# Loading a weight matrix in two pieces of 16 and 112 partitions instead of one of 128

## The chip, the cores and the metric

The program runs on one core of a Trainium2 chip. The metric is the device time of one execution in microseconds (us). The kernel before takes 677.37 us, the median of three runs from 677.31 to 677.42.

## What is computed

One decoding step for a batch of two rows x of 448 values. The result mixes attention over a cache (16 heads of 256 values, 4096 positions) with a small feed-forward block, by a gate g:

```python
g = _sigmoid((x * gate_w).sum(-1, keepdims=True))
q = (x @ wq).reshape(B, Sq, H, Dh).transpose(0, 2, 1, 3)   # wq: 448 x 4096
scores = einsum("bhqd,bhkd->bhqk", q, k_cache) * (Dh ** -0.5)
a = einsum("bhqk,bhkd->bhqd", softmax(scores), v_cache) ... @ wo
r = relu(x @ w1 + b1); b = (r * r) @ w2 + b2
return g * a + (1 - g) * b
```

All data is float32. The two caches are 134 MB each, and the four weight matrices together 21 MB.

## The kernel before

The work is cut into 16 rounds; a round takes one batch row and two heads. Per round an 8.4 MB tile of the K cache is loaded into one of two buffers (`kp0`, `kp1`) and an 8.4 MB tile of the V cache into a third (`vp`), each as 128 partitions (rows of the on-chip memory) of 64 KB. VectorE (DVE) multiplies the K tile by q in place (line 445) and sums along each row (line 450), in two halves of 8.7 us each; a maximum, two exponentials on ScalarE (ACT) and 32 matmuls with V on TensorE (PE, `values`) follow.

Nearly all loads are issued by SyncE (SP), in program order, through `load` (line 273), which issues one `dma_start` and registers what it writes. SP waits, before each load, until the buffer is free: before a K tile for DVE, before a V tile for PE. The class `Flow` works these waits out from the named regions that each operation reads and writes, and every load has a semaphore of its own name.

The start of the program is what the change touches. Line 303 calls the first part of `vp` the tile `wq_t`: the 448 x 4096 matrix wq, laid out as 128 partitions of seven consecutive half rows, 14,336 values or 57,344 bytes, which are contiguous in the main memory too. Line 304 is SP's first load and brings in the whole of it; line 405 is the second and brings the K tile of round 0. ACT issues four small loads meanwhile (x, gate_w and b2 to two partitions each, and b1, line 325, to sixteen partitions of 448 bytes). On PE the order is: a turn of x (line 373), the gate (396), b2 (398), b1 (400), and then 28 matmuls x @ wq (line 427, drawn as 56 in the profile), which wait for wq. Their result is scaled into `qs` (line 428) and spread into the q of rounds 0 and 1 (`make_q`). Only after the wq matmuls may SP issue the load of w1, into the same place of `vp` (line 430); w1's matmuls (line 435) stand in the same way before the first V tile. At the end come the last V tile in three pieces, w2 in four pieces, and PE's closing matmuls.

Of the kernel before, what the change touches and what calls it, by code (L numbers as in the profile page):

```python
# [10 lines left out]
PE, ACT, DVE, POOL, SP = "PE", "ACT", "DVE", "POOL", "SP"  # L11
# [12 lines left out]
class Flow:  # L24
# [22 lines left out]
    def op(self, eng, fn, r=(), w=(), give=None, take=(), dma=None):  # L47
        proc = dma or eng
        looped = eng == PE and self.body is not None
        o = Op(proc, eng, fn, give, looped)  # L50
        mine = self.ops.setdefault(proc, [])
        mine.append(o)
        o.n = len(mine)
        know = self.know[eng]
        for t in take:
            p = self.tokens[t].pop(0)
            o.takes.append((t, 16 if p.proc not in self.eng else 1))
            self.learn(know, p)
        need = {}
        for writes, regions in ((False, r), (True, w)):  # L60
            for name, lo, hi in map(self.span, regions):
                for p, a, b, wrote in self.seen.setdefault(name, []):
                    if a >= hi or b <= lo or not (wrote or writes):
                        continue
                    if p.proc == proc == PE:
                        continue
                    if know.get(p.proc, 0) < p.n and need.get(p.proc, p).n <= p.n:
                        need[p.proc] = p
        for p in sorted(need.values(), key=lambda p: -p.n):
            if know.get(p.proc, 0) >= p.n:  # L70
                continue
            assert not looped, (eng, p.proc, p.n, r, w)
            while p.give and p.proc in self.eng:
                later = [q for q in self.ops[p.proc][p.n:] if not q.give and q is not o]
                assert later, (eng, p.proc, p.n, r, w)
                p = later[0]
            p.inc = True
            o.waits.append(p)
            self.learn(know, p)
        for writes, regions in ((False, r), (True, w)):  # L80
            for name, lo, hi in map(self.span, regions):
                at = self.seen.setdefault(name, [])
                if writes:
                    at[:] = [x for x in at if not (lo <= x[1] and x[2] <= hi)]
                at.append((o, lo, hi, writes))
        o.know = dict(know)
        if give:
            self.tokens.setdefault(give, []).append(o)
        if looped:
            if self.passes == 1:  # L90
                self.body.append(o)
            else:
                first = self.body[self.at]
                assert first.takes == o.takes and not o.waits, (first.takes, o.takes)
                self.at += 1
        else:
            self.order[eng].append(o)
        return o
# [84 lines left out]
def gated_mix_kernel(nc, x, k_cache, v_cache, wq, wo, w1, b1, w2, b2, gate_w, out):  # L183
    P = 128
    B, H, S, DH = k_cache.shape
    D = x.shape[-1]
    F = w1.shape[1]
    N = H * DH
    XR = 7
# [10 lines left out]
    QB = 512  # L200
    NQ = N // QB
# [4 lines left out]
    BUSY = (8, 12, 3, 1)  # L206
    SLOTS = (0, 16, 104)
    LEAD = 4
    HJ = HG * DH // P
    HP = P // HG  # L210
    HN = HG * DH
# [4 lines left out]
    op = flow.op  # L216

    def sb(name, *shape):
        return nc.alloc_sbuf_tensor(name, shape, F32).ap()

    def bank(name):
        return nc.alloc_psum_tensor(name, (P, 512), F32).ap()

    kp = [sb(f"kp{n}", P, NK * DH) for n in range(2)]
    vp = sb("vp", P, NK * DH)
    wo_t = sb("wo", P, HJ * D)
    b1T = sb("b1T", P, FC)
# [8 lines left out]
    xT = sb("xT", P, 2, XC, 2, B)  # L236
# [20 lines left out]
    rl_t = [sb(f"rl{n}", P, HG * B, 2) for n in range(2)]  # L257
    oTw = sb("oTw", P, HJ, B)
    oT2 = o2_w.rearrange("p (b j) -> p j b", b=B)[:, :HJ // 2, :]
    oTn = on_w.rearrange("p (b j k) -> p j k b", b=B, k=2)[:, :NJ, :, :]  # L260

    po_t = [bank(f"po{n}") for n in range(2)]
# [10 lines left out]
    def load(eng, sem, dst, src, w, r=(), give=None):  # L273
        e = flow.eng[eng]
        op(eng, lambda: e.dma_start(dst, src), r=r, w=w, dma=sem, give=give)  # L275

    def place(t, lo=0, hi=NK * DH):
        return ("vp" if t is vp else "kp1" if t is kp[1] else "kp0", lo, hi)
# [22 lines left out]

    by7 = "(r k) (s n) -> (r k s) n"
    wq_t = vp[:, :D * N // P]
    load(SP, "wq", wq_t, wq.rearrange(by7, k=XR, s=2).rearrange("(p k) n -> p (k n)", k=XR), [place(vp, 0, D * N // P)])

    start_at = kp[1][:B, :4 * D + XC * P]

# [58 lines left out]
    def mms(calls):  # L366
        def run():
            for out_, lhsT, rhs, start, stop in calls:
                i = t_.matmul(out_, lhsT, rhs, start=start, stop=stop, skip_group_check=True)  # L369
            return i  # L370
        return run

    op(PE, mms([(pxv[:, c, :], xr[:, c].rearrange("b r s -> b (r s)"), ident[:B, :B], True, True) for c in range(XC)]),
       r=[xr_r, "ident"], w=["sm"])
# [6 lines left out]
    def times_x(out_, t, width, n):  # L381
        calls = []
        for a in range(XR):
            c, half = divmod(a, 2)
            for k in range(n):
                calls.append((out_[32 * k:32 * k + 2 * B, :width], xT[:, half, c].rearrange("p s b -> p (s b)"),
                              t[:, (a * n + k) * width:(a * n + k + 1) * width], a == 0, a == XR - 1))
        return mms(calls)
# [35 lines left out]
        c = col(i)  # L424
        op(ACT, lambda: s_.activation(sel, c, AF.Copy), r=["ident"], w=["sel"], give="q")

    op(PE, times_x(po_t[1], wq_t, QB, NQ // 2), r=["xT", place(vp, 0, D * N // P)], w=["po1"])
    op(ACT, lambda: s_.activation(qs, po_t[1], AF.Copy, scale=scale), r=["po1"], w=["qs"])
    w1_t = vp[:, :D * F // P]
    load(SP, "w1", w1_t, w1.rearrange(by7, k=XR, s=2).rearrange("(p k) n -> p (k n)", k=XR), [place(vp, 0, D * F // P)])  # L430
# [5 lines left out]
    for k in range(FB // 2):  # L436
        op(ACT, lambda k=k: s_.activation(h_sb[:, k * D:(k + 1) * D], ph[32 * k:32 * k + 2 * B, :D], AF.Copy),
           r=["ph"], w=[("shared", k * D, (k + 1) * D)])
    load_k(1)

    def times_q(i, half, lo, hi):
        t, a, q = kp[i % 2], half * J, q_of[i]
        kt = rows(t)[:, a + lo:a + hi, :]
        at = [place(t, (a + lo) * DH, (a + hi) * DH)]
        vec(lambda: v_.tensor_tensor(kt, kt, q.unsqueeze(1).to_broadcast([P, hi - lo, DH]), op=ALU.mult), at + [f"q{i % 3}"], at)  # L445
# [14 lines left out]
    def maximum(i, token=False):  # L460
        s = s_t[i % 2]
        vec(lambda: v_.tensor_reduce(m, s, axis=AX.X, op=ALU.max), [f"s{i % 2}"], ["m"], give="m" if token else None)
        op(PE, mms([(mt[k * PH:(k + 1) * PH, :PH], m.to_broadcast([P, PH]), ident[:, k * PH:(k + 1) * PH], True, True)
                    for k in range(2)]), r=["m", "ident"], w=["mt"], take=["m"] if token else ())
# [56 lines left out]

    o_w = shared.rearrange("r (s j k p) -> r s j k p", s=2, j=HJ // 2, k=HG)

    def turn_wide(u):
        ptv = sm[:, :HJ * HG * B].rearrange("p (j c) -> p j c", c=HG * B)
        po, rl = po_t[0], rl_t[u % 2]
        pv = po.rearrange("r (s p j) -> r s j p", s=2, j=HJ)
        for lo in range(0, HJ, HJ // 2):
            for s in range(2):
                op(ACT, lambda s=s, lo=lo: s_.activation(o_w[:, s], pv[:, s, lo:lo + HJ // 2].unsqueeze(2).to_broadcast([P, HJ // 2, HG, HP]),  # L530
                                              AF.Copy), r=["po0"], w=[("shared", s * HN // 2, (s + 1) * HN // 2)])
            ov = o_w.rearrange("r s j k p -> r s j (k p)")
            op(PE, mms([(ptv[:, lo + j, :], ov[:, s, j, :], rl[:, :, s], s == 0, s == 1)
                        for j in range(HJ // 2) for s in range(2)]), r=["shared", f"rl{u % 2}"], w=["sm"])
        if u < NG - 2:
            op(ACT, lambda: s_.activation(po, zero.to_broadcast([P, 512]), AF.Copy), r=["zero"], w=["po0"])
        for k in range(HG):
            at = slice(k * HP, (k + 1) * HP)
            op(ACT, lambda k=k, at=at: s_.activation(oTw[at], ptv[at, :, B * k:B * k + B], AF.Copy), r=["sm"], w=[("oTw", k, k + 1)])  # L539
# [135 lines left out]
    maximum(i + 1)  # L675
    times_q(i + 2, 0, 0, LEAD)
    softmax(i + 1)
    times_q(i + 2, 0, LEAD, J)
    values(i, vt)
# [15 lines left out]
    maximum(i + 1)  # L695
    times_q(i + 2, 0, 0, LEAD)
    norm(NG - 1)
    softmax(i + 1)
    times_q(i + 2, 0, LEAD, J)
    values(i, vt)  # L700
# [61 lines left out]
```

## Time and profile before

| what | value |
|---|---|
| median of three runs | 677.37 us |
| the profiled execution, its own time | 677.36 us |
| its span, first to last instruction | 675.9 us |
| read from the main memory | 289.56 MB, 428 GB/s over the span |
| DVE busy | 571.4 us (85%) |
| PE busy | 252.1 us (37%) |
| ACT busy | 43.0 us (6%) |
| wq: from SP's issue to landing | 19.5 us |

Times in the rows are microseconds from the span's start, unless a column is marked ns. PE is TensorE's matmuls and PEld its weight loads; an engine's name with a q is its instruction queue, so SPq rows are loads being issued. Every helper that issues a matmul or a load has one line, so L369 is any matmul and L275 any load; the tile names tell them apart (`vp<-in_A_wq_dram` is wq into `vp`). In the sliced rows a digit is a busy share in tenths. The DMA share is the mean over the core's 16 DMA engines. A DMA packet is counted in the slice in which it starts, with all its bytes, so short windows show bursts.

### The profile page before, as it was taken

What the parts mean: (1) busy time and instruction counts of PE and PEld (TensorE: products, weight loads), DVE (VectorE), ACT (ScalarE), POOL (GpSimd) and SP (SyncE); (2) the same over time, 40 slices, a digit from 0 to 9 for tenths busy, and PEclk for the clock granted to TensorE, in tenths of its full rate; (3) what the DMA queues carried; (4) which work ended last, traced back from release to release, by engine and by line L of the source; (5) the groups of instructions that cost most, each with busy time, mean ns of one, the idle gap of its engine ahead of it and who ended that gap; (6) DMA issues with size and microseconds to landing.
All of it is one profiled execution on the core that took longest, in us unless ns stands there. A gap on an engine that the chain in (4) does not pass through costs nothing.

```text
span 675.9 us, 3913 instructions
## 1 busy us (share of the span) xinstructions
PE 252.1 (37%) x1716; PEld 87.3 (13%) x1716; DVE 571.4 (85%) x149; ACT 43.0 (6%) x143; POOL 0.7 (0%) x6
## 2 busy tenths in 40 slices
PE   2522350502305751140505455050421480421598
PEld 1100210100101510010101411010100140100223
DVE  3069999999999895979979896897979899999930
ACT  0001000000100201010000201000010110000000
POOL 0000000000000000000000000000000000000000
PEclk9956575665758567585856578565575856565789
DMA  9999999999999999999999999999999999999997
GB/s 381 430 434 435 435 434 434 434 434 435 434 434 434 423 435 434 430 434 434 434 434 434 442 431 434 434 434 430 427 430 434 418 468 430 430 431 434 397 434 316
DMA packets 6688, 289.73 MB, mean 429 GB/s; under 512 B 783, under 2 KB 917, under 8 KB 1557
## 3 DMA queue, kind: packets, MB, share of 16 engines
q1 hardware_dynamic: 6632, 289.55, 99.3%
q8 instruction: 9, 0.15, 0.1%
q10 hardware_dynamic: 44, 0.02, 0.0%
q14 instruction: 3, 0.02, 0.0%
HBM read 289.56 MB, written 0.01 MB: 428 GB/s over the span
## 4 chain that ended last, share of the span: by engine, by line
DMA 49%; DVE 31%; PE 3%; SPq 0%; issue 0%; DVEq 0%
DMA kp<-in_A_k_cache_dram 32%; DVE s L450 15%; DVE kp L445 15%; DMA vp<-in_A_v_cache_dram 11%; DMA kp<-in_B_w_dram 6%; PE po L369 3%; SPq L275 0%; PE fin L369 0%; PE mt L369 0%; DVE shared L733 0%; DVEq L155 0%; DVE nb L472 0%
## 5 line engine op out<-in xcount | busy, mean ns | idle before, releaser
L445 DVE TENSOR_TENSOR kp<-kp,q 128x8192 f32<-128x8192 f32 (+2 forms) x34 | 278.2, 8183 | 49.5 <-DMA kp<-in_A_k_cache_dram 49.5
L450 DVE TENSOR_REDUCE s<-kp 128x32 f32<-128x8192 f32 x32 | 277.9, 8686 | 1.1
L369 PE MATMUL po<-vp,pw 128*16 128x512 f32 (+1 forms) x960 | 135.9, 729 | 229.9 <-PEq L153 209.3
L369 PEld LDWEIGHTS po<-vp,pw 128*16 128x16 f32 (+1 forms) x960 | 31.0, 110 | 331.5 <-issue 307.9
L369 PE MATMUL mt<-ident,m 128*64 128x64 f32 x64 | 7.3, 318 | 140.5 <-PEq L153 86.7
L369 PE MATMUL sm<-rl,shared 128*128 128x8 f32 (+1 forms) x120 | 25.3, 348 | 9.4 <-ACT shared L530 8.1
L369 PEld LDWEIGHTS sm<-rl,shared 128*128 128x128 f32 x120 | 24.7, 313 | 11.6 <-DVE rl L503 4.6
L369 PE MATMUL acc<-wo,oTw 128*2 128x448 f32 x48 | 25.0, 687 | 2.5 <-ACT oTw L539 2.5
L369 PEld LDWEIGHTS mt<-ident,m 128*64 128x64 f32 x64 | 4.8, 191 | 154.4 <-issue 98.5
L491 ACT ACTIVATE pw<-zero 128x128 f32<-128x128 f32 x12 | 3.7, 311 | 326.1 <-PE po L369 326.1
L479 ACT ACTIVATE pw<-s,nb 64x64 f32<-64x64 f32 x32 | 11.1, 348 | 167.2 <-DVE nb L472 167.0
L733 DVE COPY shared<-fin 128x112 f32<-128x112 f32 x1 | 0.3, 275 | 20.1 <-PE fin L369 20.1
L369 PE MATMUL ph<-vp,xT 128*4 128x448 f32 x28 | 7.0, 664 | 16.8 <-DMA vp<-in_B_w_dram 16.8
L472 DVE TENSOR_REDUCE nb<-mt 128x1 f32<-128x64 f32 x16 | 3.6, 224 | 10.4 <-PE mt L369 10.4
L369 PE MATMUL pq<-qs,sel 128*64 128x256 f32 x48 | 12.3, 594 | 0.0
L369 PE MATMUL po<-kp,pw 128*8 128x512 f32 x64 | 10.0, 785 | 5.9 <-DMA kp<-in_A_v_cache_dram 5.9
L369 PE MATMUL po<-vp,xT 128*4 128x512 f32 x56 | 7.6, 699 | 1.4 <-DMA vp<-in_A_wq_dram 1.4
L421 ACT ACTIVATE q<-pq 128x256 f32<-128x256 f32 x16 | 6.1, 383 | 21.6 <-PE pq L369 21.4
L501 DVE RECIPROCAL rc<-sm 128x8 f32<-128x8 f32 (+1 forms) x5 | 1.0, 196 | 7.7 <-PE sm L369 7.7
L530 ACT ACTIVATE shared<-po 128x512 f32<-128x512 f32 x12 | 6.5, 591 | 11.4 <-PE sm L369 11.4
L369 PEld LDWEIGHTS acc<-wo,oTw 128*2 128x2 f32 x48 | 4.5, 99 | 20.7 <-issue 18.0
L369 PE MATMUL ph<-kp,ones_pp 128*16 128x512 f32 x48 | 6.7, 593 | 0.0
(77 smaller groups left out, 77.6 us busy)
## 6 DMA issues: line engine op xcount, KB each, us to landing
vp<-in_A_wq_dram SPq DMA_DIRECT2D x1, 7168.0 KB, 19.5
wo<-in_A_wo_dram SPq DMA_DIRECT2D x3, 1792.0 KB, 46.5
vp<-in_A_v_cache_dram SPq DMA_DIRECT2D x1, 4096.0 KB, 24.1
vp<-in_B_w_dram SPq DMA_DIRECT2D x1, 3136.0 KB, 19.1
vp<-in_A_v_cache_dram SPq DMA_DIRECT2D x1, 3072.0 KB, 31.0
wo<-in_A_wo_dram SPq DMA_DIRECT2D x2, 896.0 KB, 33.9
kp<-in_B_w_dram SPq DMA_DIRECT2D x1, 1792.0 KB, 36.9
vp<-in_A_v_cache_dram SPq DMA_DIRECT2D x1, 1024.0 KB, 33.1
```

What stands on the lines that cost most here:

```text
L369: i = t_.matmul(out_, lhsT, rhs, start=start, stop=stop, skip_group_check=True)
L421: op(ACT, lambda: s_.activation(t, pq[:, :DH], AF.Copy), r=["pq"], w=[f"q{i % 3}"])
L445: vec(lambda: v_.tensor_tensor(kt, kt, q.unsqueeze(1).to_broadcast([P, hi - lo, DH]), op=ALU.mult), at + [f"q{i % 3}"], at)
L450: vec(lambda: v_.tensor_reduce(s[:, at], rows(t)[:, at, :], axis=AX.X, op=ALU.add), [place(t, half * HALF, (half + 1) * HALF)], [(f"s{i % ...
L472: vec(lambda: v_.tensor_reduce(nb, mt[:, :PH], axis=AX.X, op=ALU.max, negate=True), ["mt"], [f"nb{i % 2}"])
L479: op(ACT, lambda: s_.activation(pw[at, :, 2 * c:2 * c + 2], s[at].rearrange("p (m s) -> p m s", s=2), AF.Exp, bias=nb[at], accum_out=rs[at ...
L491: op(ACT, lambda: s_.activation(at, zero.unsqueeze(2).unsqueeze(3).to_broadcast([P, NK // 2, 2, 2]), AF.Copy), r=["zero"], w=[("pw0", 2 * ...
L501: vec(lambda: v_.reciprocal(c, sm[:, :B * n].rearrange("p (k b) -> p k b", b=B)), ["sm"], ["rc"])
L530: op(ACT, lambda s=s, lo=lo: s_.activation(o_w[:, s], pv[:, s, lo:lo + HJ // 2].unsqueeze(2).to_broadcast([P, HJ // 2, HG, HP]), AF.Copy), ...
L733: vec(lambda: v_.tensor_copy(y4, fin[:, :DQ]), ["fin"], [("shared", 0, DQ)])
```

## The change

The one load of wq becomes two on the same queue, of the same 57,344 bytes per partition: partitions 0 to 15, and then partitions 16 to 127. Each has its own semaphore and its own region name, and the wq matmuls read both regions.

```diff
+    WQ_FIRST = 16
...
     wq_t = vp[:, :D * N // P]
-    load(SP, "wq", wq_t, wq.rearrange(by7, k=XR, s=2).rearrange("(p k) n -> p (k n)", k=XR), [place(vp, 0, D * N // P)])
+    wq_v = wq.rearrange(by7, k=XR, s=2).rearrange("(p k) n -> p (k n)", k=XR)
+    wq_at = [place(vp, 0, D * N // P)]
+    for lo, hi in ((0, WQ_FIRST), (WQ_FIRST, P)):
+        load(SP, f"wq{lo}", wq_t[lo:hi], wq_v[lo:hi], [f"wq{lo}"])
+        wq_at.append(f"wq{lo}")
...
-    op(PE, times_x(po_t[1], wq_t, QB, NQ // 2), r=["xT", place(vp, 0, D * N // P)], w=["po1"])
+    op(PE, times_x(po_t[1], wq_t, QB, NQ // 2), r=["xT", *wq_at], w=["po1"])
```

The head of SP's queue, in the order in which SP issues its loads, with partitions x values per partition, reads before:

```order
L275 DMA vp<-in_A_wq_dram 128x14336
L275 DMA kp<-in_A_k_cache_dram 128x16384
L275 DMA vp<-in_B_w_dram 128x6272 [waits s_PE]
L275 DMA kp<-in_A_k_cache_dram 128x16384 [waits s_DVE]
L275 DMA vp<-in_A_v_cache_dram 128x16384 [waits s_PE]
```

and now:

```order
L276 DMA vp<-in_A_wq_dram 16x14336
L276 DMA vp<-in_A_wq_dram 112x14336
L276 DMA kp<-in_A_k_cache_dram 128x16384
L276 DMA vp<-in_B_w_dram 128x6272 [waits s_PE]
L276 DMA kp<-in_A_k_cache_dram 128x16384 [waits s_DVE]
```

One load more stands at the head; what follows is in the same order behind the same waits (`in_B_w` is w1 here). On PE the first instructions, with the semaphores that they wait for, were:

```order
L369 MATMUL sm<-gd,ones_pp 128x4 [waits s_DVE]
L369 MATMUL acc<-kp,gd 2x448 [waits s_b2]
L369 MATMUL ph<-kp 128x112 [waits s_b1]
L369 MATMUL po<-vp,xT 4x512 [waits s_wq]
L369 MATMUL po<-vp,xT 4x512 x27
```

and are now:

```order
L374 MATMUL sm<-gd,ones_pp 128x4 [waits s_DVE]
L374 MATMUL acc<-kp,gd 2x448 [waits s_b2]
L374 MATMUL ph<-kp 128x112 [waits s_b1]
L374 MATMUL po<-vp,xT 4x512 [waits s_wq16,s_wq0]
L374 MATMUL po<-vp,xT 4x512 x27
```

The first wq matmul waits for two semaphores in place of one, and nothing changed its place. DVE, ACT and GpSimd have the same instructions in the same order.

## The prediction, made before the changed kernel ran

> **What bounds the kernel now.** I read the page's slices first, then the chain of work that ended last, and last the first 60 us of the timeline, where the change lies. The page gives the span, the mean share of the 16 DMA engines in 40 slices of 17 us, and what they moved:
>
> ```profile
> span 675.9 us, 3913 instructions
> DMA  9999999999999999999999999999999999999997
> GB/s 381 430 434 435 435 434 434 434 434 435 434 434 434 423 435 434 430 434 434 434 434 434 442 431 434 434 434 430 427 430 434 418 468 430 430 431 434 397 434 316
> q1 hardware_dynamic: 6632, 289.55, 99.3%
> DMA 49%; DVE 31%; PE 3%; SPq 0%; issue 0%; DVEq 0%
> ```
>
> The transfers are never idle, and they run on a plateau of 434 GB/s whatever they bring (K, V, w1, wo), which is 27.1 GB/s for each of 16 engines. SP's queue, q1, holds 99.3% of all engine time. 289.55 MB at 434 GB/s are 667 us, so all but 9 us of the span is this one stream. The chain names DVE for 31%, but DVE's share there is cover, not cause:
>
> ```profile
> 111.97 8.69 DVE kp L445
> 120.69 8.69 DVE s L450
> 129.38 8.61 DVE kp L445
> 138.01 8.70 DVE s L450
> 146.72 37.08 DMA kp<-in_A_k_cache_dram
> ...
> 634.28 38.65 DMA kp<-in_B_w_dram
> 672.93 0.04 issue
> 672.98 0.98 PE fin L369 x24
> 673.95 0.02 issue
> 673.98 0.28 DVE shared L733
> ```
>
> Four DVE passes free a K buffer (start, duration, what), its refill is issued, and the next K tile lands 37 us later; the stream moves other tiles throughout those DVE passes. The end is set by w2, the last load, landing at 672.9, and 1.3 us of PE and DVE behind it. A microsecond that the stream loses anywhere, with no wait elsewhere to take it up, is a microsecond at the end.
>
> **The start, where the change lies.** The timeline's rows for SP, and for those who wait for the first loads:
>
> ```profile
> 0.74 0.39 SPq L275 DMA_DIRECT2D vp<-in_A_wq_dram  x1
> 1.20 0.41 SPq L275 DMA_DIRECT2D kp<-in_A_k_cache_dram  x1
> ...
> 18.11 0.76 PE L369 MATMUL ph<-kp 16*128 16x112 f32 x2 [2.63 <-DMA kp<-in_B_b_dram]
> ...
> 20.24 7.55 PE L369 MATMUL po<-vp,xT 128*4 128x512 f32 x56 [1.36 <-DMA vp<-in_A_wq_dram]
> ...
> 27.86 0.33 SPq L275 DMA_DIRECT2D vp<-in_B_w_dram  x1
> 28.24 0.44 SPq L275 DMA_DIRECT2D kp<-in_A_k_cache_dram  x1
> ...
> 39.64 8.69 DVE L445 TENSOR_TENSOR kp<-kp,q 128x8192 f32<-128x8192 f32 x1 [20.14 <-DMA kp<-in_A_k_cache_dram]
> ```
>
> wq lands at 20.2, its matmuls end at 27.8 and let w1's load go at 27.86; the first K tile lands at 39.6 and starts DVE. Now the DMA view of the 17 us in which wq moves, and two windows at the start:
>
> ```profile
> GB/s 1223 944 0 0 0 0 270 1889 0 0 0 140 2042 0 0 0 270 1889 0 0 0 139 2028 0 0 0 135 2024 0 0 0 135 2026 0 0 0 270 1889 0 0
> DMA packets 172, 7.36 MB, mean 433 GB/s; under 512 B 38, under 2 KB 44, under 8 KB 44
> q1 hardware_dynamic: 128, 7.34, 103.1%
> q10 hardware_dynamic: 44, 0.02, 0.4%
> ```
>
> ```profile
> 0.00:1.50 1.50, 0.00 (x0) 0.00 (x0) 0.56 (x3) 0.00 (x0) 0.70 (x6) 1.00 0.00 0
> 1.50:18.50 17.00, 4.48 (x14) 2.74 (x14) 5.29 (x25) 1.49 (x2) 0.00 (x0) 1.00 1.04 433
> ```
>
> wq is 128 packets of 57,344 bytes, one per partition, and they start in eight bursts 2.1 us apart: 16 engines in step, eight rows each, 57,344 / 27,100 = 2.12 us a row, 16.9 us in all. The last column of the windows is GB/s: nothing moves in the first 1.5 us.
>
> The q10 row tells how a 16-row load is dealt out. ACT's four loads bring six packets of 1,792 bytes (three loads to two partitions) and sixteen of 448 (b1). The row counts 44, so 22 are completion packets: 2 + 2 + 2 + 16. Each engine that takes part reports once, so b1's sixteen rows went to sixteen engines, one row each. wq's first piece has sixteen rows as well: one each, and then 112 / 16 = seven rows an engine.
>
> **The change, part by part.**
>
> *The extra issue and packets.* SP issues one load more, 0.39 us by the wq row, so the K load goes at about 1.6 instead of 1.20. Its bytes stand behind 16.9 us of wq in the same queue, which hides that; without this cover it would cost the 0.39. One more completion packet per engine: all 44 packets of q10 take 0.4% of 17 us, 0.07 us. PE's second wait is for a load queued ahead of the other, so it is already over when the first ends. I take nothing for all three.
>
> *A quicker beginning.* A load of sixteen rows may begin sooner. SP starts to issue at 0.74 and no byte moves before 1.5, so there is at most 0.8 us to gain. Nothing shows that the delay grows with the rows: I take nothing, and keep -0.8 as an end.
>
> *The first sixteen rows.* No row of the trace shows a large load to sixteen neighbouring partitions; every large load reaches all 128. What the rows allow: 16 engines at a common 27.1 GB/s, each bringing eight rows of 128, which is what one would see if the on-chip memory had sixteen ways in, eight rows behind each, and every engine a way to itself. If the sixteen ways are real, sixteen neighbours can lie behind all of them (one row each, 2.1 us as now) or behind as few as two (eight rows each, 8 x 2.12 = 16.9 us). So the piece costs between 0 and 14.8 us over its 2.1. I take the middle in ratio, between four and eight ways, on the careful side: four ways, four rows through each, 8.5 us, a loss of **6.3 us**. While this lasts every engine is held by its own row, and three quarters of the ways stand empty.
>
> [...]
>
> *The 112 rows.* Seven rows an engine are 14.8 us if no two engines meet. [...] The ends: no meeting, 0; every row shared by two engines throughout, 29.6 us, a loss of 14.8. The trace has no row nearer to one of them; I take half, **7.4 us**. The loss counts with the engine that is last, because wq has landed only when all sixteen report, and because no later load gives an engine less to do to catch up.
>
> [...]
>
> *What the delay does behind it.* wq lands at 20.2 + 13.7 = 33.9, its matmuls end at 41.5, and w1 is issued then. The first K tile, queued behind wq, now lands at 39.6 + 13.7 = 53.3: the stream still has 11.8 us of work when w1 comes, as before (27.86 against 39.64). An engine that is early by up to the 7.4 us doesn't run dry; if one did, it would not delay the late ones. DVE, which waited 20.1 us for the first K tile, waits 33.8. In every later round DVE and PE wait for tiles of the same stream, so the whole schedule moves by the delay. Could it be won back? Only in the 9 us in which the stream is below its plateau, and there SP waits for work that itself waited for a late tile (the row below); those gaps move along.
>
> ```profile
> SPq L275 <- PE po L369: 409.3, 14, 37.3
> ```
>
> **The sum**, against the profiled execution's own 677.36 us (675.9 of span and 1.5 around it, and within 0.01 of the median of 677.37): 677.4 + 6.3 + 7.4 = **691.1 us**, 2.0% slower.
>
> **The rivals.**
>
> *Not slower: no ways are shared.* If the 27.1 GB/s is the pace of a DMA engine and the memory takes sixteen neighbouring rows as fast as any, both pieces run at 434 GB/s, one row and seven, and the bytes are the same. Also if the split left each row with the engine that has it now, nothing would change. Then only the beginning counts: 677.4 less 0 to 0.8, 676.6 to 677.4. It decides from the point where the second burst starts: 2.1 us after the first, as now, and it is this rival. For it: nothing in the trace shows a shared way. Against it: the plateau is the same for rows of 57, 64 and 14 KB and while DVE is at work, as a fixed limit on one side of the engines would give, and the present dealing is one in which such a limit can't show.
>
> *Only the first piece pays.* The 112 rows may be dealt out so that engines don't meet: 677.4 + 6.3 = 683.7 us. Against it: seven doesn't divide into groups of eight.
>
> *The engines meet far more often.* If the rows are dealt out so that several engines walk through the same neighbourhood together, the 112 rows go as slowly as the first sixteen, four rows to a way: 7 x 8.5 = 59.2 us instead of 14.8, a loss of 44.4, and the end at 677.4 + 6.3 + 44.4 = 728 us. In between, rows strewn without order would have about three engines on the busiest way at times: twice 14.8 lost, 713 us.
>
> **How the numbers follow.** The forecast, with a loss from 9 to 20 us, has 54%. Only the first piece (a loss of 1.4 to 9) has 14%; both pieces near their upper ends (20 to 30 us) 12%; more than 30 us 10%; no sharing 10%. The range reaches from only the first piece less the quicker beginning, 683.7 - 0.8, rounded down to 682, to both upper ends, 677.4 + 14.8 + 14.8 = 707. It leaves out no sharing and the losses above 30 us, 20% together. A measurement of this kernel can tell about 0.2% (1.35 us) from no change. The quicker beginning alone, 0.8 us, stays below that; faster gets 3%, within 0.2% 7%, slower 90%.
>
> **What would show it.** In the DMA view from 1.6 us on, the second burst of wq packets should start some 8.5 us after the first instead of 2.1, with 16 packets and 0.9 MB before it, and the next bursts should fall out of step. The 16-row load should land near 11 us and the 112-row load near 34; the first DVE pass over K should start near 53 instead of 39.64. After that the slices should be at 434 GB/s as now, and every later row 13 to 15 us late, to the end. The prediction is wrong if the bursts stay in step, if wq lands before 25, or if the first K pass is late by the sum and the end is not.

## The result and the profile after

The changed kernel takes 695.46 us (median of four runs, 695.36 to 696.2) against 677.34 for the kernel before beside it: 18.1 us more, a ratio of 1.0271 with a 95% interval from 1.0258 to 1.0284. The forecast was 691.1, with a range from 682 to 707. The profiled execution took 695.52 us, its span 694.2.

The page's slices after the change:

```profile
span 694.2 us, 3915 instructions
DMA  9999999999999999999999999999999999999997
GB/s 160 264 415 427 424 431 453 438 423 423 434 427 457 418 426 438 446 434 430 423 434 430 417 452 430 438 438 438 430 423 434 434 439 427 430 439 430 406 435 296
q1 hardware_dynamic: 6648, 289.55, 99.1%
```

The digits of the DMA row say nothing: the engines count as busy as ever. The loss stands in the row below it. The first two slices of 17 us move 160 and 264 GB/s where before they moved 381 and 430; from the third on the stream is back on its plateau. A busy DMA engine may be one that is held up.

The DMA view from 1.6 us on, in 40 slices of 1 us, shows the bursts in which wq's packets start:

```profile
DMA  9900000990009200912921952997229728913919
GB/s 749 172 0 0 0 0 0 633 289 0 0 1 869 57 0 0 860 57 57 746 57 57 745 115 57 229 459 172 57 57 631 172 57 262 590 66 131 918 66 786
DMA packets 247, 10.18 MB, mean 254 GB/s; under 512 B 70, under 2 KB 76, under 8 KB 76
```

749 + 172 GB/s over 1 us are sixteen packets of 57,344 bytes, the first piece. The second burst comes 7 us after the first instead of 2.1, and those after it come at 12, 16, 19, 22 to 23, 26 and 30 us, three to five us apart. Nearly all sixteen engines stay in step, on a slower beat. The rows of the timeline that answer to those of before:

```profile
0.74 0.86 SPq L276 DMA_DIRECT2D vp<-in_A_wq_dram  x2
...
1.64 0.48 SPq L276 DMA_DIRECT2D kp<-in_A_k_cache_dram  x1
...
25.33 0.76 PE L374 MATMUL ph<-kp 16*128 16x112 f32 x2 [4.30 <-DMA kp<-in_B_b_dram]
...
39.00 8.79 PE L374 MATMUL po<-vp,xT 128*4 128x512 f32 x56 [12.90 <-DMA vp<-in_A_wq_dram]
47.87 0.35 SPq L276 DMA_DIRECT2D vp<-in_B_w_dram  x1
...
48.26 0.43 SPq L276 DMA_DIRECT2D kp<-in_A_k_cache_dram  x1
...
58.32 8.69 DVE L450 TENSOR_TENSOR kp<-kp,q 128x8192 f32<-128x8192 f32 x1 [31.61 <-DMA kp<-in_A_k_cache_dram]
```

The wq matmuls begin at 39.00 instead of 20.24, 18.8 us late, and DVE's first pass over K at 58.32 instead of 39.64, 18.7 us late. All of the delay is there before the first round begins. The small loads on ACT's queue are late as well (b1's matmul at 25.33 instead of 18.11), but still ahead of wq, so nobody waits longer for them.

The two groups of DMA issues that replace wq's one (19.5 us from issue to landing before; the last column is that time):

```profile
vp<-in_A_wq_dram SPq DMA_DIRECT2D x1, 6272.0 KB, 37.7
...
vp<-in_A_wq_dram SPq DMA_DIRECT2D x1, 896.0 KB, 10.8
```

### The profile page after: what moved, and what is told of

Its sections match the earlier page's. It is cut to its first block, busy times and chain, and to the rows that moved or that the text cites. A ratio compares the mean times of both kernels' runs of the same rounds, so it can differ in the third digit from the quotient of the medians.

```text
span 694.2 us, 3915 instructions
## 1 busy us (share of the span) xinstructions
PE 254.9 (37%) x1716; PEld 87.8 (13%) x1716; DVE 571.3 (82%) x149; ACT 42.9 (6%) x143; POOL 0.7 (0%) x6
## 4 chain that ended last, share of the span: by engine, by line
DMA 40%; DVE 25%; PE 5%; issue 0%; SPq 0%; DVEq 0%
DMA kp<-in_A_k_cache_dram 26%; DMA vp<-in_A_v_cache_dram 15%; DVE s L455 13%; DVE kp L450 12%; PE po L374 4%; PE ph L374 1%; PE fin L374 1%; PE sm L374 0%; PE mt L374 0%; SPq L276 0%; DVE shared L738 0%; DVEq L155 0%; DVE nb L477 0%
## 5 line engine op out<-in xcount | busy, mean ns | idle before, releaser
L374 PE MATMUL po<-vp,pw 128*16 128x512 f32 (+1 forms) x960 | 138.1, 739 | 223.1 <-PEq L153 201.0
```

## The experiments

I took the loss as two terms, one for the sixteen rows and one for the 112, and tested each by itself. In most kernels below wq is loaded in one piece as before, and one more load, which nothing uses, goes ahead of it on SP's queue into a free part of the second K buffer. Its cost is the difference of two medians from the same chip. The theory is that of the prediction: partitions that are neighbours share ways into the on-chip memory. The rival is the source: neighbouring rows of the main memory, read at one time, might collide there.

### Sixteen rows, and where they come from and go to

The extra load, in four forms of destination and source; each kernel has one of the four `load` lines, just ahead of the load of wq:

```diff
+    wq_v = wq.rearrange(by7, k=XR, s=2).rearrange("(p k) n -> p (k n)", k=XR)
+    pt_, pv_ = kp[1][:, 3072:16384], wq_v[:, :13312]
+    at_ = [place(kp[1], 3072, 16384)]
+    load(SP, "probe", pt_[0:16], pv_[0:16], at_)      # p16
+    load(SP, "probe", pt_[0:P:8], pv_[0:16], at_)     # p16_dst8
+    load(SP, "probe", pt_[0:16], pv_[0:P:8], at_)     # p16_src8
+    load(SP, "probe", pt_[16:P], pv_[16:P], at_)      # p112
```

*Neighbours to neighbours (p16).*

> The kernel before, with one load ahead of wq on SP's queue that brings nothing that is used: rows 0 to 15 of wq, 53,248 bytes each (0.85 MB), into partitions 0 to 15 of the second K buffer. wq itself is loaded in one piece as before. The bytes alone cost 1.97 us (53,248 / 27,100). Ways theory (neighbouring partitions share ways into the on-chip memory, four rows to a way): 7.9 us, so 685.2 us, and the 16-row load lands some 9 us after its issue. Source theory (sixteen neighbouring rows of the main memory are read slowly): the same here. If it is only the number of loads: 679.4.

*The same rows, spread over the partitions (p16_dst8).*

> The same extra load from the same sixteen neighbouring rows of wq, but into partitions 0, 8, 16, ... 120 of the second K buffer. Ways theory: the rows lie behind at least twice as many ways, so 2.0 to 3.9 us, 679.3 to 681.3 us. Source theory: as with partitions 0 to 15, since the reading is the same, some 685 us.

*Rows from afar into neighbouring partitions (p16_src8).*

> The same extra load into partitions 0 to 15, but of rows 0, 8, 16, ... 120 of wq, spread over the whole matrix in the main memory. Ways theory: as with neighbouring rows, some 685 us, since the writing is the same. Source theory: the rows lie as far apart as those that the 128-row load reads at one time, so 2.0 us, 679.3 us.

Measured: p16 684.83 against 677.33, 7.5 us; p16_dst8 681.73, 4.4 us; p16_src8 684.84, 7.5 us. For sixteen rows the source rival falls: spreading the source by eight rows changes nothing, spreading the destination saves 3.1 us. The sixteen neighbours go at 0.85 MB in 7.5 us, 114 GB/s, a quarter of the plateau of 434.

### The 112 rows by themselves

> The kernel before, with one unused load ahead of wq: rows 16 to 127 of wq, 53,248 bytes each (5.96 MB), into partitions 16 to 127 of the second K buffer; wq in one piece as before. The bytes alone cost 13.8 us (691.1). If the 112-row piece loses by itself what it lost in the changed kernel (its rows took 26.6 us there instead of 14.8, a loss of 11.8, or 11.0 for the shorter rows): 702.1 us. If it loses only because its engines come out of the 16-row piece at different times, or only the forecast's 7.4: 691 or 698.

Measured: 703.12 against 677.33, 25.8 us where the bytes alone take 13.8. So the 112 rows need no sixteen-row piece ahead of them to go slowly. This is the larger term.

### Two loads that both reach all partitions

```diff
+    CUT = D * N // P // 8
+    for lo, hi in ((0, CUT), (CUT, D * N // P)):
+        load(SP, f"wq{lo}", wq_t[:, lo:hi], wq_v[:, lo:hi], [place(vp, lo, hi)])
```

> wq in two loads on SP's queue as in the changed kernel, of the same 0.9 and 6.4 MB, but cut along the columns: the first eighth of each of the 128 partitions, then the rest. Ways theory: both loads reach all partitions and each engine has its way to itself: no cost, 677.3 us within 0.5. If two loads, their second issue or second wait cost something by themselves: the part of the 18.1 us that is due to them.

Measured: 677.28 against 677.46, a ratio of 0.9996 with an interval from 0.9987 to 1.0006. Two loads, two issues and two waits cost nothing that can be measured; what costs is the cut between partitions. The sooner landing of a small first piece (its 896 KB were there 4.9 us after the issue) gains nothing either.

### Two halves

The changed kernel with `WQ_FIRST = 64`.

> The changed kernel with the cut at 64 instead of 16: partitions 0 to 63, then 64 to 127. Ways theory, with half of the ways behind each half of the partitions: each piece takes as long as the whole did, 33.8 us for both instead of 16.9, 694.3 us. If only few rows (sixteen) are slow, or shares that don't fit groups of eight: four rows an engine fit, 677 us.

Measured: 696.37 against 677.46, 18.9 us. The two halves together take an estimated 16.9 + 18.9 = 35.8 us, so each of them, on the average, about as long as the whole took. Four rows an engine don't help: the 677 us of that rival is out.

### How the rows are dealt out

```diff
+    load(SP, "probe", pt_[16:P:7], pv_[0:16], at_)                            # p16_dst7
+    load(SP, "probe", pt_[0:120], pv_[0:120], at_)                            # p120
```

*The first row of each block of seven (p16_dst7).*

> The kernel before, with an unused load of rows 0 to 15 of wq (53,248 bytes each) ahead of wq, into partitions 16, 23, 30, ... 121 of the second K buffer: the first row of each block of seven, as far as the 112-row piece is dealt out in such blocks. They lie as spread as a step of eight (which cost 4.4 us) or more. [...] Coupled ways (an engine that waits for a shared way holds others back): all sixteen rows slow, 3.3 us as the first rows of the 112-row load were, 680.7 us or more.

*120 rows (p120).*

> The kernel before, with an unused load of rows 0 to 119 of wq (53,248 bytes each, 6.39 MB) ahead of wq, into partitions 0 to 119 of the second K buffer. The bytes alone cost 14.7 us (692.1). If only sixteen neighbours meet, or if a load of 120 rows is dealt out as one of 128 is, each way to one engine: 15.7 us, 693.1. [...]

Measured: p16_dst7 681.31 against 677.46, 3.9 us. p120 710.32, 32.9 us for 14.7 us of bytes. That is a little over twice the 15.7 us of eight rows an engine at the full pace. Fifteen engines take part, as I read the packets: the first burst below has fifteen of 53,248 bytes (14 in the 1498 of its first slice, one in the 106), and q1 counts 6767 packets in all where the kernel before has 6632, so 120 rows and 15 more, while the sixteen rows of p16_at32 add 16 and 16 (6664). Which rows an engine got is not in the views; that they are blocks of eight neighbours is an estimate from the fifteen engines and the cost. The DMA view of p120 from 1.6 us on, in slices of 0.5 us:

```profile
DMA  9050500999500055995500059955000099550000
GB/s 1498 0 106 0 115 0 0 639 639 213 106 0 0 0 115 111 970 320 107 107 0 0 0 116 959 426 107 107 0 0 0 0 548 958 106 106 0 0 0 0
DMA packets 117, 4.24 MB, mean 212 GB/s; under 512 B 32, under 2 KB 38, under 8 KB 38
```

The bursts come 4.2 us apart: 53,248 bytes at 12.8 GB/s for every engine, half of 27.1 and a little less. The small numbers show something more. 106 and 107 are one packet of 53,248 bytes in a slice, but 115 and 116 are one of 57,344: those are wq's. I take them for the rows of the sixteenth engine, which has no share in the 120 and goes on to wq at once. They start in slices 5, 15 and 24, 4.5 to 5 us apart, where they took 2.12 before. It too goes at half its pace beside a load in which it has no part.

### Sixteen rows at a step of four, and 64 in the middle

Three more places: sixteen partitions at a step of four, from 32 and from 28, and the 64 from 32 to 95. That some of them would be fast was my estimate; no run before these shows it.

```diff
+    load(SP, "probe", pt_[32:96:4], pv_[0:16], at_)                           # p16_at32
+    load(SP, "probe", pt_[28:92:4], pv_[0:16], at_)                           # p16_at28
+    load(SP, "probe", pt_[32:96], pv_[0:64], at_)                             # p64_mid
```

> The kernel before, with an unused load of rows 0 to 15 of wq (53,248 bytes each) ahead of wq, into partitions 32, 36, 40, ... 92 of the second K buffer. [...] If sixteen rows on sixteen engines are slow wherever they lie, as partitions 0, 8, ... 120 and 16, 23, ... 121 were: 681.3 to 681.7 us.

> The same load, four partitions lower: 28, 32, ... 88. [...] Coupled ways (all engines go at the pace of the most crowded way): all sixteen rows take some 3.3 us and the second burst comes as one, 681.3 us. [...]

> The kernel before, with an unused load of rows 0 to 63 of wq (53,248 bytes each, 3.41 MB) ahead of wq, into partitions 32 to 95 of the second K buffer. [...] If what counts is that only half of the partitions are reached (as with 0 to 63, where both halves together took 18.9 us more than the whole): some 16.6 us, 694 us.

Measured against 677.47: p16_at32 679.86, 2.4 us; p16_at28 680.66, 3.2 us; p64_mid 685.86, 8.4 us. Sixteen rows at a step of four from 32 cost their bytes (2.0 us) and 0.4 us. Sixty-four partitions from 32 to 95 cost theirs (7.9 us) and 0.5, which is the full pace, where the two halves of 64, from 0 and from 64, go at half (35.8 us for both). So the place decides: the same sixteen rows cost 7.5 us in partitions 0 to 15 and 2.4 us here, and a load that reaches half of the partitions can go at the full pace. Which partitions share a way, the runs don't show beyond these places.

The 0.4 us is not the price of a load more, for the column cut has one more too and cost nothing. SP's first issue takes 0.64 us in p16_at32 and 0.40 in p16, and the first rows start some 0.4 us later (in slice 3 instead of slice 1 of the views below, in p16_at28 too). The timeline's rows, p16 first and then p16_at32:

```profile
0.74 0.40 SPq L275 DMA_DIRECT2D kp<-in_A_wq_dram  x1
0.73 0.64 SPq L275 DMA_DIRECT2D kp<-in_A_wq_dram  x1
```

p16_dst8 and p16_dst7 have the longer issue as well (0.64 and 0.65); p16 and p112 have the short one (0.40 both), and the first rows of p16_src8 start as soon as those of p16 (2396 GB/s in the 0.2 us from 1.7 in both), so there nothing is to be taken off. Why some issues take longer, no run here shows. Less the 0.4, p16_dst8 cost 4.0 us, about two row times.

The starts of the packets, in slices of 0.25 us from 1.6 us on: first the sixteen neighbours (p16), then the step of four from 32 (p16_at32), then the one from 28 (p16_at28), last the sixteen of p16_dst7.

```profile
GB/s 1292 852 0 1065 0 213 0 0 0 0 0 0 0 0 0 0 0 0 0 0 0 0 0 0 229 229 703 918 229 0 459 459 459 0 0 0 0 0 0 0
DMA packets 56, 1.78 MB, mean 178 GB/s; under 512 B 20, under 2 KB 24, under 8 KB 24
```

```profile
GB/s 7 7 1065 213 426 1704 0 0 0 0 0 7 1169 1147 459 918 0 0 0 0 231 1618 694 1156 0 0 0 0 0 688 1606 459 918 0 0 0 0 229 1376 918
DMA packets 135, 4.25 MB, mean 425 GB/s; under 512 B 54, under 2 KB 60, under 8 KB 60
```

```profile
GB/s 14 0 1278 426 426 1278 0 0 0 0 0 237 1154 459 229 459 688 7 7 459 0 0 2 1154 233 923 235 690 0 231 231 229 1147 229 688 688 229 0 229 229
DMA packets 124, 3.62 MB, mean 362 GB/s; under 512 B 54, under 2 KB 60, under 8 KB 60
```

```profile
GB/s 14 0 1065 426 639 1065 213 0 0 0 0 0 7 466 14 459 688 688 229 1147 0 0 0 0 0 2 923 1156 925 694 0 0 0 0 459 918 918 1147 229 0
```

229 GB/s in 0.25 us is one wq packet. In the first view the second burst begins after 6 us; in the second after 2.5, and the next ones 2 to 2.25 us later. In the third, fourteen packets begin from slice 12 to slice 17, 2.25 us and more after the first burst, and the last two (459) only in slice 20, 4.25 us after it. I take those two for engines that meet; they leave the other fourteen alone at first. This speaks for independent ways, in which a meeting costs only those who meet, and against the first form of the coupled theory, in which all engines go at the pace of the most crowded way. But the next burst of p16_at28 begins in slice 24, 2.75 to 3 us after the one before, instead of 2.1: once the two are late and the others have gone on to wq, all slow down.

In the fourth view no engine keeps the pace: the sixteen next packets begin from slice 14 to slice 20, each 2.75 to 3.5 us after its place in the first burst, where those of p16_at32 came 2 to 2.5 us after theirs. Which of these rows meet, no view shows. If not all of them do, engines which meet nobody are slowed with those that meet; the slower burst of p16_at28 and the sixteenth engine of p120 point the same way. The costs alone (3.2 us for p16_at28, 3.9 for p16_dst7) would not show it, because a late row can cost up to 2.0 us at the end with independent ways too.

## Why the prediction was right, and where it was not

**The bound.** Right. A stream that loses 18.7 us at the start ends 18.1 us late; almost nothing was won back elsewhere. From the third slice on the stream runs at its pace of before.

**The small edits at nothing.** Right: the column cut has the same two issues and two waits, and two packets a row, and costs nothing. The K load's issue at 1.64 instead of 1.20 was hidden, as was said. The quicker beginning brought nothing.

**The first sixteen rows, 6.3 us.** Right that the place among the partitions costs (p16 7.5 us, p16_at32 2.4), and nearly right in size. p16 cost 7.5 us; less the 2.0 of its bytes the meeting costs 5.5, or 6.0 us for wq's longer rows (57,344 / 53,248). The 114 GB/s of p16 is near a quarter of the plateau, as four ways of sixteen would give, and that the choice of four came out right was in part luck: the prediction took it as a middle between two ends and not from a row. The piece landed 10.8 us after its issue at 0.74, so at 11.5, near 11 as forecast, but the second burst came after 7 us and not 8.5.

**The 112 rows, 7.4 us.** Right that they lose by themselves, wrong in who pays for it, and too small; this is the step that failed: "The trace has no row nearer to one of them; I take half". No run shows the 7.4 us. In its place, p112 cost 25.8 us; less 13.8 for the bytes it lost 12.0, or 13.0 us for wq's rows, close to the upper end of 14.8 that the prediction gave ("every row shared by two engines throughout"). With 6.0 for the first piece that makes 19.0, against 18.1 measured: the two terms account for all of the loss and overshoot it by 0.9 us. So the split between them is known to about a microsecond (in the changed kernel itself the second burst was 4.9 us late). I had taken it that a meeting costs those who meet, and that the last engine sets the loss. In the runs others are slowed too: in p120 the engine that has no share in the load (4.5 to 5 us a row instead of 2.12), and in p16_dst7 all sixteen (2.75 to 3.5 us to the next packet, where p16_at32 has 2 to 2.5). Why, they don't show. It isn't the reading of neighbouring rows, which p16_src8 excludes for sixteen rows; for the 112 the source was not varied. No run tried what holds the engines, and the dealing in blocks of seven is itself an inference.

**What the delay does behind it.** w1 was issued at 47.87 with K's landing at 58.32, so the stream had 10.4 us in hand (11.8 forecast): the wq matmuls took 8.79 us instead of 7.55. It never ran dry. In the middle of the run the delay was 17.4 us (the K pass that stood at 265.52 stands at 282.90), and 18.1 at the end; this difference I didn't follow.

**What would show it.** Bursts 8.5 and not 2.1 us apart: yes, 7. Bursts out of step: no. They stayed in step on a slower beat, which the prediction had named as a sign that it is wrong; I read it as the mark of a coupling. The 112 rows' landing near 34: wq's matmuls began at 39.0. First pass near 53: 58.3. So the forecast of "slower" and the range held, with the wrong picture of how the 112 rows lose.

**The rivals.** No shared ways is out (p16 7.5 us against 2.4 in p16_at32). Only the first piece is out (p112, 12.0 us over its bytes). Engines meeting four to a way in the 112 rows is out: 25.8 us and not some 55. The delay fell in the case that was forecast, 9 to 20 us.

## What to carry to other kernels

In a kernel that its transfers bind, look at the bytes that each slice moves, not at the share of busy DMA engines: held-up engines count as busy (here 90% or more in a slice that moved 160 GB/s). Cut a load along its columns, where each piece still reaches all 128 partitions, and not along its partitions; the first cost nothing here, the second 18 us on a load of 17. If only some partitions can be loaded, measure which: 32 to 95 cost 8.4 us for 7.9 us of bytes, while 0 to 63 and 64 to 127 took an estimated 35.8 us where the whole took 16.9.

## What I had not expected of the hardware

A load that leaves out a few partitions can be half as fast: 120 partitions took 32.9 us where 128 such rows at the plateau are 15.7, so eight rows fewer doubled the time. And an engine slows down beside a load in which it has no part: in p120 the sixteenth engine, without a share in the 120 rows as I read the packets, brought wq's rows in 4.5 to 5 us instead of 2.12. In p16_dst7 none of the sixteen kept the pace (2.75 to 3.5 us to the next packet).
